# A spectral filter and two MLPs in one kernel: the filter's units regrouped, most of the last transform moved into its loop, weight preparation re-timed

## The chip, the core and the metric

The kernel runs on one core of a Trainium2 chip. The core has a matrix engine (PE, TensorE), three elementwise engines (DVE or VectorE, ACT or ScalarE, POOL or GpSimd) and a queue engine (SP, SyncE) that here issues every DMA. Each engine works through its own list of instructions in order and waits where an operand is not there yet. The metric is the device time of one execution in microseconds (us); the profile's span runs from its first to its last instruction.

## What is computed

```
X = rfft(x, axis=1);  Y = X * (filt_r + 1j*filt_i);  y = irfft(Y, n=3008)   # x: 2 x 3008 x 256
h = y.reshape(6016, 256) @ moe_w_in;  g = maximum(0.01*h, h);  z = g @ moe_w_out   # 256 -> 2048 -> 256
h = z @ moe2_w_in;  r = maximum(h, 0);  out = (r*r) @ moe2_w_out                   # 256 -> 2048 -> 256
```

All of it is float32. The weights arrive as 64-bit words.

## The kernel before, in words

**Filter.** The 3008-point transform is done as 47 x 64 by matrix products. The data go in 32 *units*, each 16 channels of one of the two batches. The loop over s (lines 680 to 723) is a software pipeline, one unit per step: `load_x` (DMA), `stage_a` (PE product `pa`), `stage_r` (DVE transpose `bin`), `stage_b` (PE product `px`), `stage_s` (ACT copies `xc`, DVE multiplies by `fr`), `stage_2` (POOL multiplies by `fi`), `stage_y` (for units in `SWAP` the two products are added, on DVE for those in `SWAP_V`, else on POOL), `stage_i` (PE product `zps`, two of them for units that are not in `SWAP`), `stage_t` (DVE transpose into `zin`). The sign of `fi` is applied in place, by `sign_f` on DVE or POOL, or by `sign_k` on ACT. `units` (line 529) alternates the batches, so each `fr` tile serves two neighbouring units.

**Last transform.** It has 32 *items* (h, j): half h of the channels and 376 tokens j. `stage_o` does four PE products `pi`, `stage_w` copies the result to the first tokens' tile `x0` or to `xo`, from where SP writes it to the DRAM tensor `xt`. An item can run when all units of its half and batch are in `zin`. Before, the 16 items of the first half run in the loop from step 19 on and in its drain, the other 16 in `fill()` (lines 743 to 756) after the loop's buffers are given back.

**MLPs.** A *macro* is a pair of token blocks (512 or 480 tokens each), a *panel* 256 of the 2048 hidden units; one *step* is one panel of one macro. There are 96 steps, 48 in each layer. `up(i, part)` does the seven block products of a step in three passes each (21 PE instructions `ph`), `down` 24 more (`py`). Of a step's results DVE forms `v`, `u` and three `h` in a fixed order, ACT applies the activation twice (`g` and the rounded `gp`), POOL forms the rest `gp` as a difference. PE's list runs one step ahead with `up`: the product into a `ph` bank that `u` or `v` reads is waited for.

**Side work.** Two tick clocks set where other work stands in the engines' lists: `begin(clock, steps, table, start)` gives each named operation a due tick, `tick` records what is due. The loop ticks "F" four times a step; `up` ticks "M" (and F) eight times a step, so a step of the MLP is `TM = 8` ticks. On them lie: `narrow_w`, which turns a panel's 64-bit words into float32 (ten DVE operations, lines 213 to 228, with `add`, `sums` and the split into high and low halves on POOL, DVE and ACT), for panels 0 to 3 of layer one at `STARTS` (clock F), panels 4 to 7 at `STARTS_1`, and the eight panels of layer two from `STARTS_2` on, one every 32 ticks (clock M; these go to DRAM, and `split_w` reads them back in layer two, late by `LATE`); and `macro_steps`, which prepares the operands of the next macro: `load`, the differences `sum0` to `sum3` (POOL, line 333), the halves `hi_` (ACT) and `lo_` (line 344; five on DVE, two on POOL), from 24 ticks before the macro's first step to 2 behind it. The macros of layer one begin at ticks 32, 128, 192, 256 and 320 (a first macro is split in two visits, the second of which reloads its operands).

```
for d in [d for d in due[c] if d[0] <= clock[c]]:
    due[c].remove(d)
    d[1]()
```

Of the kernel before, what the change touches and what calls it, by code (L numbers as in the profile page):

```python
# [9 lines left out]
F32 = mybir.dt.float32  # L10
# [10 lines left out]
NB = 2  # L21
# [18 lines left out]
WARM = 12  # L40


SWAP = (3, 7, 9, 11, 12, 15, 16, 17, 18, 19, 20, 21, 22, 23, 24, 25, 26, 27, 28, 29, 30, 31)
SWAP_V = (3, 16, 17, 18, 20, 21, 25, 26, 27, 29, 30)


FI = ((2, 4, 2), (4, 8, 2), (8, 16, 7))
SGN = (1, 2)
SIGN = ((4, 8, 4, 4), (8, 16, 9, 3))

H0 = 3
DRAIN = (2, 2, 2, 2)
FILLS = 13
OUT_V = (0, 1, 2, 3, 4, 5, 6, 7, 9, 15)

FIN = (0, 0)

TM = 8
STARTS = (-10, 34, 72, 112)
STARTS_1 = (0, 16, 32, 56)
STARTS_2 = 80


HALF = 4
# [13 lines left out]
    low1=17, load1=17, add1=18, out_o=19, out_i=26,  # L82
)

LATE = 20
SPLIT_W = dict(load=16, hi_i=18, hi_o=19, lo_i=20, lo_o=23)
FIRST = dict(
    hi_t1=-13, hi_b11=-13, lo_t1=-13, lo_b11=-13, sum1=-12, hi_b21=-12, lo_b21=-11, hi_t2=-11, lo_t2=-10, sum2=-9,
    sum3=-8, hi_t3=-8, lo_t3=-7, hi_t4=-7, lo_t4=-6, hi_b22=-6, lo_b22=-5,
)  # L90
MACRO = dict(
    load=-24, sum0=-16, sum1=-15, sum2=-12, hi_b11=-11, sum3=-9, hi_b21=-8, hi_t2=-8, lo_b11=-8, lo_t2=-8,
# [9 lines left out]
    N2=(),  # L102
    S=("lo_o",),
    M=("lo_b11", "lo_b21", "lo_t2", "lo_t3", "lo_t4"),
    M0=("lo_t2", "sum1", "sum2", "sum3", "lo_t4"),
)


# [43 lines left out]
def fft_filter_then_two_mlps(  # L152
# [343 lines left out]
    with ExitStack() as fctx:  # L496
# [5 lines left out]
        ps_z = actx.enter_context(tc.tile_pool(name="ps_z", bufs=1, space=PS))  # L502
        ps_x = actx.enter_context(tc.tile_pool(name="ps_x", bufs=2, space=PS))
        ps_a = actx.enter_context(tc.tile_pool(name="ps_a", bufs=3, space=PS))
        xin_p = actx.enter_context(tc.tile_pool(name="xin", bufs=4, side="right"))
        f_p = actx.enter_context(tc.tile_pool(name="flt", bufs=4, side="right"))
        s_p = actx.enter_context(tc.tile_pool(name="fs", bufs=3, side="right"))

# [17 lines left out]
        for _ in range(WARM):  # L526
            nc.tensor.matmul(warm_ps, warm[:, :P], warm, start=True, stop=True)

        units = [(b, q) for q in range(NU) for b in range(NB)]
        fr_sb = {}  # L530
        z10 = [z1_p.tile([P, P * NJ], F32, tag="z10", name="fi0")]
        fi_sb = [
# [10 lines left out]
            xin[s] = t  # L543

        def load_fr(q):
            fr_sb[q] = f_p.tile([P, UC, NK], F32, tag="fr", name="fr")
            nc.sync.dma_start(fr_sb[q], fr[:, q * UC : (q + 1) * UC, :])

        def load_fi(q0, q1):
# [81 lines left out]
                )  # L631
            pis[h, j] = pi

        def stage_w(h, j, eng):
# [6 lines left out]
            if h == 0:  # L641
# [27 lines left out]
        nc.sync.dma_start(cs, c_cs)
        load_w(0, 0, 1)  # L670
        load_x(3)
        load_fr(1)
        load_fi(1, 2)
        load_x(4)
        nc.sync.dma_start(dd, c_dd)
        n = len(units)
        h0 = w0 = 0
        for k, t in enumerate(STARTS):
            begin("F", narrow_w(0, k, f"F{k}"), NARROW_F, t)
        for s in range(n + 4):  # L680
# [12 lines left out]
            tick("F")
# [29 lines left out]
            tick("F")
        while w0 < NO:
            if h0 < NO:
                stage_o(0, h0, ps_a, "pa")
# [14 lines left out]
        h1 = iter(range(NO))  # L741

        def fill():
            j = next(h1)
            stage_o(1, j, ps_y, f"py{j % 4}")
            stage_w(1, j, nc.vector if j in OUT_V else nc.scalar)
# [102 lines left out]
```

## Time and profile before

| | |
|---|---|
| time, median of 3 runs | 1163.13 us (1162.51 to 1165.67) |
| the profiled execution: its time / its span | 1165.77 us / 1163.1 us |
| PE busy | 1117.3 us, 96% of the span |
| PE weight load, DVE, ACT, POOL busy | 883.9, 652.8, 649.8, 765.6 us |
| mean granted TensorE clock | 0.993 of full speed |
| DMA | 80.12 MB in all, mean 69 GB/s |

A busy share is a mean over stages with different limits. The filter and its last transform take the first 131 us, the two MLPs the rest. A row of the timeline gives the start, the time and the instruction, merged with its like (x6: six of them), and in brackets how long the engine had been idle and what ended that.

### The profile page before, as it was taken

To read this page: it belongs to the slowest core of one execution; us is meant where nothing else is said; L and a number is where in the kernel's file an instruction comes from. 1 tells how busy PE (TensorE), PEld (TensorE's weight loads), DVE (VectorE), ACT (ScalarE), POOL (GpSimd) and SP (SyncE) were. 2 spreads that over 40 slices of the span, in tenths; PEclk is the share of its full clock that TensorE was granted. 3 is DMA by queue.
4 is the path that set the end of the run, shared out by engine and by line. 5 is a ranking of instruction groups with operands and counts; after the bars stand their busy time and mean duration, and the time that the engine had idled before them with its cause. 6 is when DMAs were issued, how large, how long until landed. Compare 5 with 4: busy or idle time off the path is not lost.

```text
span 1163.1 us, 14072 instructions
## 1 busy us (share of the span) xinstructions
PE 1117.3 (96%) x4800; PEld 883.9 (76%) x4800; DVE 652.8 (56%) x870; ACT 649.8 (56%) x1209; POOL 765.6 (66%) x616
## 2 busy tenths in 40 slices
PE   7899978999899899899899999999999999999998
PEld 3466866888688688678688788788888788788887
DVE  6899788565854854855744643533534434435432
ACT  3855456554554554555555765655656555656554
POOL 3785598777757857756767876745647547557544
PEclk9999999999999999999999999999999999999999
DMA  7653712116022022023032030010100200200100
GB/s 229 189 158 117 265 54 78 55 56 239 20 82 95 23 84 86 19 80 96 1 111 87 28 106 38 31 40 1 63 11 1 71 1 1 71 1 1 37 1 34
DMA packets 35238, 80.12 MB, mean 69 GB/s; under 512 B 4544, under 2 KB 14880, under 8 KB 35040
## 3 DMA queue, kind: packets, MB, share of 16 engines
q1 hardware_dynamic: 35168, 79.25, 20.6%
q8 instruction: 37, 0.61, 0.2%
q14 instruction: 33, 0.27, 0.1%
HBM read 51.31 MB, written 27.92 MB: 68 GB/s over the span
## 4 chain that ended last, share of the span: by engine, by line
PE 76%; DVE 10%; ACT 4%; issue 4%; POOL 3%; DMA 2%; SPq 0%; DVEq 0%; POOLq 0%; ACTq 0%
PE py L463 38%; PE ph L368 34%; DVE xop L344 3%; PE pi L629 1%; POOL gp L391 1%; ACT g L381 1%; PE pa L571 1%; PE px L583 1%; DMA xin<-in_x 1%; ACT xop L338 1%; DVE u L402 1%; DVE wm L213 1%; DVE wi L222 1%; PE zps L613 1%; ACT gp L382 1%
## 5 line engine op out<-in xcount | busy, mean ns | idle before, releaser
L391 POOL TENSOR_TENSOR gp<-g,gp 128x512 fp32r<-128x512 f32 (+1 forms) x384 | 502.6, 1318 | 340.0 <-ACT gp L382 102.4
L463 PE MATMUL py<-gp,wao 128*128 128x512 f32 (+1 forms) x1152 | 287.8, 391 | 0.3 <-POOL gp L391 0.3
L463 PE MATMUL py<-gp,wbo 128*128 128x512 f32 (+1 forms) x1152 | 288.0, 392 | 0.0
L368 PE MATMUL ph<-xop,wai 128*128 128x512 f32 (+1 forms) x1008 | 259.2, 394 | 20.5 <-DVE v L402 11.6
L368 PE MATMUL ph<-xop,wbi 128*128 128x512 f32 (+1 forms) x1008 | 254.9, 391 | 8.7 <-DVE u L402 8.7
L463 PEld LDWEIGHTS py<-gp,wbo 128*128 128x128 f32 x1152 | 217.2, 189 | 48.1 <-POOL gp L391 0.2
L463 PEld LDWEIGHTS py<-gp,wao 128*128 128x128 f32 x1152 | 216.5, 188 | 48.5 <-POOL gp L391 0.7
L368 PEld LDWEIGHTS ph<-xop,wai 128*128 128x128 f32 x1008 | 187.7, 188 | 69.3 <-DVE v L402 14.1
L368 PEld LDWEIGHTS ph<-xop,wbi 128*128 128x128 f32 x1008 | 187.5, 187 | 53.4 <-DVE u L402 10.4
L381 ACT ACTIVATE g<-h 128x512 f32<-128x512 f32 (+1 forms) x144 | 88.9, 617 | 133.5 <-DVE h L402 128.9
L402 DVE TENSOR_TENSOR u<-ph,p 128x512 f32<-128x512 f32 (+1 forms) x96 | 65.0, 677 | 156.4 <-PE ph L368 156.4
L402 DVE TENSOR_TENSOR v<-ph,p 128x512 f32<-128x512 f32 (+1 forms) x96 | 65.0, 677 | 136.8 <-PE ph L368 64.7
L389 ACT ACTIVATE g<-h 128x512 f32<-128x512 f32 (+1 forms) x144 | 89.0, 618 | 85.6 <-DVE h L398 84.1
L387 ACT ACTIVATE r<-ph 128x512 f32<-128x512 f32 (+1 forms) x48 | 28.2, 587 | 106.5 <-PE ph L368 106.5
L390 ACT ACTIVATE gp<-h 128x512 fp32r<-128x512 f32 (+1 forms) x144 | 87.4, 607 | 0.0
L382 ACT ACTIVATE gp<-h 128x512 fp32r<-128x512 f32 (+1 forms) x144 | 87.3, 607 | 0.0
L381 ACT ACTIVATE g<-ph 128x512 f32<-128x512 f32 (+1 forms) x48 | 28.2, 587 | 97.9 <-PE ph L368 97.9
L398 DVE CUSTOM_DVE_ANT_0 h<-ph,p 128x512 f32<-128x512 f32 (+1 forms) x48 | 32.6, 680 | 86.8 <-PE ph L368 86.8
L402 DVE TENSOR_TENSOR h<-ph,p 128x512 f32<-128x512 f32 (+1 forms) x48 | 32.7, 680 | 73.7 <-PE ph L368 73.7
L421 ACT ACTIVATE p<-ph 128x512 f32<-128x512 f32 (+1 forms) x96 | 54.7, 570 | 1.5 <-PE ph L368 1.5
L601 POOL TENSOR_TENSOR t<-xc,fi 128x384 f32<-128x384 f32 x32 | 35.8, 1121 | 21.1 <-ACT xc L591 16.5
L344 DVE TENSOR_TENSOR xop<-x,xop 128x512 fp32r<-128x512 f32 (+1 forms) x33 | 41.0, 1243 | 10.4 <-ACT xop L338 10.4
(200 smaller groups left out, 1146.3 us busy)
## 6 DMA issues: line engine op xcount, KB each, us to landing
wraw<-in_w SPq DMA_DIRECT2D x32, 512.0 KB
xin<-in_x SPq DMA_DIRECT2D x32, 160.0 KB
xt<-xo SPq DMA_DIRECT2D x26, 188.0 KB
yt<-o SPq DMA_DIRECT2D x16, 256.0 KB
x<-yt SPq DMA_DIRECT2D x4, 1024.0 KB
out<-o SPq DMA_DIRECT2D x16, 256.0 KB
w<-wi SPq DMA_DIRECT2D x8, 448.0 KB
wi<-w SPq DMA_DIRECT2D x8, 448.0 KB
```

The source lines that it names most:

```text
L344: eng.tensor_tensor(t[:, 1, :n], x_f32[v][name], t[:, 0, :n].bitcast(F32), ALU.subtract)
L368: nc.tensor.matmul(ph[:, :n], w[:, i, k], x[:, j, :n], start=(first and a == 0), stop=(a == 2), skip_group_check=True)
L381: nc.scalar.activation(g[:, :n], h[:, :n], AF.Prelu, alpha=0.01)
L382: nc.scalar.activation(t[:, 0, :n], h[:, :n], AF.Prelu, alpha=0.01)
L389: nc.scalar.activation(g[:, :n], h[:, :n], AF.Square)
L390: nc.scalar.activation(t[:, 0, :n], h[:, :n], AF.Square)
L391: nc.gpsimd.tensor_tensor(t[:, 1, :n], g[:, :n], t[:, 0, :n].bitcast(F32), ALU.subtract)
L398: nc.vector._custom_dve(dve_ops.TENSOR_ADD_SAT, out=t[:, :n], in0=ph[:, :n], in1=s[:, :n], s0=F32_MAX, s1=0.0)
L402: nc.vector.tensor_tensor(t[:, :n], ph[:, :n], s[:, :n], ALU.add)
L421: nc.scalar.activation(p1[:, :n], ph[0][:, :n], AF.Copy)
L463: nc.tensor.matmul(acc[c, t][:, :n], w[:, j, 2 * f + c], g[:, k, :n], start=(p == p0 and f == t and a == 0), stop=(p == p1 - 1 and f != t ...
L601: nc.gpsimd.tensor_tensor(t2, xc, fi_of(units[s][1], units[s][1] + 1), ALU.mult)
```

## The change

Units are ordered by four groups of eight: half h, then batch b, then the eight units q of that half (`GU = 8`). So the first group's items can run from step 11 on, and 24 of the 32 items lie in the loop, one a step; `FILLS = 8` remain behind it. Each `fr` tile is now needed by units eight steps apart (nine buffers instead of four) and `fr` and `fi` of the first eight units are loaded one unit at a time. The first weight panel is no longer loaded ahead of everything, and `STARTS` is 20 ticks later for panel 0. Three of the first macro's differences move into the loop on DVE. In the MLPs `STARTS_1`, `STARTS_2` and `LATE` are new numbers. The count of PE instructions stays the same.

```
-SWAP_V = (3, 16, 17, 18, 20, 21, 25, 26, 27, 29, 30)
+SWAP = (9, 10, 11) + tuple(range(13, 32))
+SWAP_V = (10, 15, 18, 21, 24, 27, 30)
-FI = ((2, 4, 2), (4, 8, 2), (8, 16, 7))
-SGN = (1, 2)
-SIGN = ((4, 8, 4, 4), (8, 16, 9, 3))
+FI = ((8, 12, 5), (12, 16, 6))
+SIGN_K = 8
+SGN = (1, 3, 5, 7)
+SIGN = ((8, 16, 9, 3),)
+GU = 8
-DRAIN = (2, 2, 2, 2)
-FILLS = 13
-OUT_V = (0, 1, 2, 3, 4, 5, 6, 7, 9, 15)
+FILLS = 8
+OUT_V = (8, 10, 11, 13, 15)
-STARTS = (-10, 34, 72, 112)
-STARTS_1 = (0, 16, 32, 56)
-STARTS_2 = 80
+STARTS = (10, 42, 75, 108)
+STARTS_1 = (0, 32, 48, 64)
+STARTS_2 = 96
-LATE = 20
+LATE = (12, 12, 12, 20, 20, 20, 20, 20)
...
-    M0=("lo_t2", "sum1", "sum2", "sum3", "lo_t4"),
+    M0=("lo_t2", "lo_t4"),
...
-        units = [(b, q) for q in range(NU) for b in range(NB)]
+        units = [(b, q) for h in range(2) for b in range(NB) for q in range(h * GU, (h + 1) * GU)]
...
-        load_w(0, 0, 0)
         load_x(0)
+        nc.sync.dma_start(cb, c_cb)
         load_x(1)
...
+            if s < n - 3 and units[s + 3][0] == 0:
+                q = units[s + 3][1]
+                load_fr(q)
+                if q < SIGN_K:
+                    load_fi(q, q + 1)
+            if s in (1, 3):
+                load_w(0, 0, s // 2)
...
-            if s > n // 2 + H0 and w0 < h0:
-                stage_w(0, w0, nc.scalar)
+            if w0 < h0:
+                stage_w(*items[w0], nc.scalar)
                 w0 += 1
                 if w0 == 5:
                     sum_macro(FIRST_V, 0, nc.gpsimd)
+                if w0 - NO in (4, 5, 6):
+                    sum_macro(FIRST_V, w0 - NO - 3, nc.vector)
...
-            if s >= n // 2 + H0:
-                for k in range(1 if s < n else DRAIN[s - n]):
-                    if h0 < NO:
-                        stage_o(0, h0, ps_a, "pa")
-                        h0 += 1
+            if s >= GU + H0 and h0 < len(items) - FILLS:
+                stage_o(*items[h0], ps_a, "pa")
                 h0 += 1
...
-            begin("M", split_w(1, p, "S", {}), SPLIT_W, ((NM - 1) * NP + p) * TM + (LATE if p >= NWA - 1 else 0))
+            begin("M", split_w(1, p, "S", {}), SPLIT_W, ((NM - 1) * NP + p) * TM + LATE[p])
```

The lines of the changed kernel are one off (L402 is L403 there). Three places in the engines' lists follow.

**PE, from the last steps of the loop to the first products `ph` of the MLP.** `pi` are the items, four products each. Before:

```order
L571 MATMUL pa<-xin,ra 128x512
L583 MATMUL px<-bin,cb 128x384
L613 MATMUL zps_122<-t_968,ci 128x16x24
L629 MATMUL pi<-dd,zin_119 128x128 x4
L583 MATMUL px<-bin,cb 128x384
L613 MATMUL zps_123<-t_997,ci 128x16x24
L629 MATMUL pi<-dd,zin_119 128x128 x8
L613 MATMUL zps_121<-t_1024,ci 128x16x24
L629 MATMUL pi<-dd,zin_119 128x128 x4
L613 MATMUL zps_122<-t_1048,ci 128x16x24
L629 MATMUL pi<-dd,zin_679 128x128 x32
L629 MATMUL pi<-dd,zin_120 128x128 x32
```

and now:

```order
L572 MATMUL pa<-xin,ra 128x512
L584 MATMUL px<-bin,cb 128x384
L614 MATMUL zps_122<-t_1019,ci 128x16x24
L630 MATMUL pi<-dd,zin_732 128x128 x4
L584 MATMUL px<-bin,cb 128x384
L614 MATMUL zps_123<-t_1046,ci 128x16x24
L630 MATMUL pi<-dd,zin_732 128x128 x4
L614 MATMUL zps_121<-t_1075,ci 128x16x24
L630 MATMUL pi<-dd,zin_732 128x128 x4
L614 MATMUL zps_122<-t_1100,ci 128x16x24
L630 MATMUL pi<-dd,zin_732 128x128 x4
L630 MATMUL pi<-dd,zin_120 128x128 x32
```

Of the 64 products of 16 items behind the last `zps`, 32 are left (and 4 just ahead of them); the others stand in the loop's steps.

**DVE, in step 3, ahead of the macro that begins at tick 32,** from `v` to `u` of one step. `xop` are the low halves of the next macro's operands; `wb`, `wi` and `wm` belong to panel 5 of layer one. Before:

```order
L402 TENSOR_TENSOR v<-ph,p_1576 128x512
L344 TENSOR_TENSOR xop<-x,xop 128x512
L344 TENSOR_TENSOR xop<-xs,xop 128x512
L217 SCALAR_TENSOR_TENSOR wb__1561<-wraw_1405,wb__1561 128x512
L222 TENSOR_SCALAR wi_1596<-wb__1561 128x512
L344 TENSOR_TENSOR xop<-x,xop 128x512
L228 SCALAR_TENSOR_TENSOR wm<-wraw_1405,wi_1596 128x512
L402 TENSOR_TENSOR u<-ph,p_1576 128x512
```

and now:

```order
L403 TENSOR_TENSOR v<-ph,p_1556 128x512
L345 TENSOR_TENSOR xop<-x,xop 128x512
L345 TENSOR_TENSOR xop<-xs,xop 128x512
L345 TENSOR_TENSOR xop<-x,xop 128x512
L403 TENSOR_TENSOR u<-ph,p_1556 128x512
```

The three operations on panel 5 have left this gap. At the macros that begin at ticks 128, 192, 256 and 320 the same happens with the panels of layer two: before, `L344`, `L344`, `L222`, `L344`, `L228` stood between `v` and `u`, now only the three `L345`.

**POOL, ahead of the macro that begins at tick 128.** `xs` and `x` (480 wide) are the macro's differences, `wi` and `wo` the layer-two panel's sums. Before:

```order
L391 TENSOR_TENSOR gp<-g,gp 128x512 x7
L333 TENSOR_TENSOR xs<-x 128x480
L333 TENSOR_TENSOR xs<-x,xs 128x480
L391 TENSOR_TENSOR gp<-g,gp 128x512 x2
L333 TENSOR_TENSOR x<-x 128x480
L391 TENSOR_TENSOR gp<-g,gp 128x512 x2
L333 TENSOR_TENSOR xs<-x,xs 128x480
L344 TENSOR_TENSOR xop<-xs,xop 128x480
```

and now:

```order
L334 TENSOR_TENSOR xs<-x 128x480
L242 TENSOR_TENSOR wi_2536<-wi_2536 128x128
L243 TENSOR_TENSOR wi_2536<-wi_2536 128x128
L244 TENSOR_TENSOR wi_2536<-wi_2536 128x128
L245 TENSOR_TENSOR wi_2536<-wi_2536 128x128
L334 TENSOR_TENSOR xs<-x,xs 128x480
L392 TENSOR_TENSOR gp<-g,gp 128x512
L237 TENSOR_TENSOR wo_2645<-wb__2609,wm 128x512
L392 TENSOR_TENSOR gp<-g,gp 128x512
L334 TENSOR_TENSOR x<-x 128x480
L392 TENSOR_TENSOR gp<-g,gp 128x512 x2
L334 TENSOR_TENSOR xs<-x,xs 128x480
```

A panel's five POOL operations of line 237 and lines 242 to 245 now stand among the macro's differences.

## Rows read from the trace of the kernel before

**Rows 1.** Page, part 1: busy time, share, instructions.

```profile
PE 1117.3 (96%) x4800; PEld 883.9 (76%) x4800; DVE 652.8 (56%) x870; ACT 649.8 (56%) x1209; POOL 765.6 (66%) x616
```

**Rows 2.** Timeline of PE, 110 to 200 us.

```profile
114.33 16.84 PE L629 MATMUL pi<-dd,zin 128*128 128x128 f32 x128 [1.48 <-DVE zin L622]
130.93 3.74 PE L368 MATMUL ph<-xop,wai 128*128 128x512 f32 x15
...
163.94 2.96 PE L463 MATMUL py<-gp,wao 128*128 128x512 f32 x12
172.57 2.92 PE L368 MATMUL ph<-xop,wai 128*128 128x512 f32 x6 [5.66 <-DVE u L402]
...
185.20 2.97 PE L463 MATMUL py<-gp,wao 128*128 128x512 f32 x12
...
196.41 2.96 PE L463 MATMUL py<-gp,wao 128*128 128x512 f32 x12
```

**Rows 3.** Timeline of DVE, 155 to 196 us.

```profile
162.23 0.69 DVE L402 TENSOR_TENSOR v<-ph,p 128x512 f32<-128x512 f32 x1 [1.42 <-ACT p L421]
...
163.70 1.77 DVE L344 TENSOR_TENSOR xop<-xs,xop 128x512 fp32r<-128x512 f32 x1
...
171.84 0.68 DVE L402 TENSOR_TENSOR u<-ph,p 128x512 f32<-128x512 f32 x1
```

**Rows 4.** What PE waited for, 200 to 600 us: total, times, longest.

```profile
PE ph L368 <- DVE v L402: 8.8, 4, 2.3
PE ph L368 <- DVE u L402: 8.7, 4, 2.4
```

**Rows 5.** Timeline of PE at the macro of tick 128, 285 to 322 us.

```profile
290.93 2.96 PE L463 MATMUL py<-gp,wbo 128*128 128x512 f32 x12
...
301.44 2.97 PE L463 MATMUL py<-gp,wbo 128*128 128x512 f32 x12
...
316.66 4.42 PE L463 MATMUL py<-gp,wbo 128*128 128x512 f32 x12
```

**Rows 6.** Timeline of DVE at the same place.

```profile
299.86 0.68 DVE L402 TENSOR_TENSOR v<-ph,p 128x512 f32<-128x512 f32 x1
...
303.06 1.52 DVE L222 TENSOR_SCALAR wi<-wb__2736 128x512 int32<-128x512 int32 x1
...
305.68 0.68 DVE L402 TENSOR_TENSOR u<-ph,p 128x512 f32<-128x512 f32 x1
```

**Rows 7.** Timeline of PE at a change of macro in layer two, 741 to 762 us.

```profile
745.79 2.96 PE L463 MATMUL py<-gp,wbo 128*128 128x512 f32 x12
...
756.79 2.96 PE L463 MATMUL py<-gp,wao 128*128 128x512 f32 x12
```

**Rows 8.** Timeline of PE in the filter, 0 to 112 us.

```profile
6.63 3.75 PE L571 MATMUL pa<-xin,ra 94*128 94x512 f32 x4 [2.51 <-DMA xin<-in_x]
...
39.82 1.02 PE L571 MATMUL pa<-xin,ra 94*128 94x512 f32 x2
...
67.58 1.02 PE L571 MATMUL pa<-xin,ra 94*128 94x512 f32 x2
...
102.68 1.02 PE L571 MATMUL pa<-xin,ra 94*128 94x512 f32 x2
```

**Rows 9.** Windows: busy us of each engine (instructions), clock, DMA share, GB/s.

```profile
0.00:30.00 30.00, 23.43 (x57) 11.86 (x58) 19.93 (x34) 10.35 (x23) 12.54 (x16) 1.00 0.80 233
30.00:40.00 10.00, 9.36 (x28) 4.90 (x27) 6.59 (x11) 8.52 (x23) 8.34 (x9) 1.00 0.94 290
```

**Rows 10.** Windows, the same columns: eleven steps of the loop, each with an item.

```profile
67.60:102.70 35.10, 34.63 (x157) 22.53 (x156) 33.77 (x55) 19.05 (x38) 25.53 (x25) 1.00 0.45 142
```

**Rows 11.** Timeline of DVE in the filter: one operation at two places.

```profile
45.28 0.64 DVE L217 SCALAR_TENSOR_TENSOR wb__444<-wraw,wb__444 128x512 int32<-128x512 int32 x1
...
80.91 1.75 DVE L217 SCALAR_TENSOR_TENSOR wb__773<-wraw,wb__773 128x512 int32<-128x512 int32 x1
```

**Rows 12.** Timeline of POOL, 78 to 84 us.

```profile
80.53 1.58 POOL L333 TENSOR_TENSOR xs<-x 128x512 f32<-128x512 f32 x1
```

More of the change, by code (lines that the diff above doesn't have):

```diff
@@ L40 @@
 WARM = 12
-SWAP = (3, 7, 9, 11, 12, 15, 16, 17, 18, 19, 20, 21, 22, 23, 24, 25, 26, 27, 28, 29, 30, 31)
-SWAP_V = (3, 16, 17, 18, 20, 21, 25, 26, 27, 29, 30)
-FI = ((2, 4, 2), (4, 8, 2), (8, 16, 7))
-SGN = (1, 2)
-SIGN = ((4, 8, 4, 4), (8, 16, 9, 3))
+SWAP = (9, 10, 11) + tuple(range(13, 32))
[5 more added lines that the diff above has]
+GU = 8
 H0 = 3
-DRAIN = (2, 2, 2, 2)
-FILLS = 13
-OUT_V = (0, 1, 2, 3, 4, 5, 6, 7, 9, 15)
+FILLS = 8
+OUT_V = (8, 10, 11, 13, 15)
 FIN = (0, 0)
 TM = 8
-STARTS = (-10, 34, 72, 112)
-STARTS_1 = (0, 16, 32, 56)
-STARTS_2 = 80
+STARTS = (10, 42, 75, 108)
+STARTS_1 = (0, 32, 48, 64)
+STARTS_2 = 96
 HALF = 4
@@ L83 @@
 )
-LATE = 20
+LATE = (12, 12, 12, 20, 20, 20, 20, 20)
 SPLIT_W = dict(load=16, hi_i=18, hi_o=19, lo_i=20, lo_o=23)
 FIRST = dict(
-    hi_t1=-13, hi_b11=-13, lo_t1=-13, lo_b11=-13, sum1=-12, hi_b21=-12, lo_b21=-11, hi_t2=-11, lo_t2=-10, sum2=-9,
-    sum3=-8, hi_t3=-8, lo_t3=-7, hi_t4=-7, lo_t4=-6, hi_b22=-6, lo_b22=-5,
+    hi_b11=-8, hi_t2=-8, lo_b11=-8, lo_t2=-7, hi_t1=-7, lo_t1=-6, hi_b21=-5, lo_b21=-4, hi_t3=-4, lo_t3=-3, hi_t4=-2,
+    lo_t4=-1, hi_b22=-1, lo_b22=0,
 )
@@ L504, in fft_filter_then_two_mlps @@
         ps_a = actx.enter_context(tc.tile_pool(name="ps_a", bufs=3, space=PS))
-        xin_p = actx.enter_context(tc.tile_pool(name="xin", bufs=4, side="right"))
+        xin_p = actx.enter_context(tc.tile_pool(name="xin", bufs=5, side="right"))
         f_p = actx.enter_context(tc.tile_pool(name="flt", bufs=4, side="right"))
@@ L545, in load_fr @@
         def load_fr(q):
-            fr_sb[q] = f_p.tile([P, UC, NK], F32, tag="fr", name="fr")
+            fr_sb[q] = f_p.tile([P, UC, NK], F32, tag="fr", name="fr", bufs=GU + 1)
             nc.sync.dma_start(fr_sb[q], fr[:, q * UC : (q + 1) * UC, :])
@@ L632, in stage_o, with stage_w @@
             pis[h, j] = pi
-        def stage_w(h, j, eng):
+        def stage_w(h, j, eng, pi_in_loop=True):
             pi = pis.pop((h, j))[:, :, : 2 * N1]
@@ L640, in stage_w @@
                 return
-            if h == 0:
+            if pi_in_loop:
                 o = xw_p.tile([P, TO], F32, tag="xo", name="xo")
@@ L659, in fft_filter_then_two_mlps @@
         x0 = load_macro(FIRST_V, load=False).rearrange("p k t n -> p k (t n)")
-        load_w(0, 0, 0)
         load_x(0)
+        nc.sync.dma_start(cb, c_cb)
         load_x(1)
-        nc.sync.dma_start(cb, c_cb)
-        nc.sync.dma_start(sg, c_sg)
         load_fr(0)
         load_fi(0, 1)
+        nc.sync.dma_start(sg, c_sg)
         load_x(2)
@@ L669, in fft_filter_then_two_mlps @@
         nc.sync.dma_start(cs, c_cs)
-        load_w(0, 0, 1)
-        load_x(3)
         load_fr(1)
         load_fi(1, 2)
-        load_x(4)
+        load_x(3)
+        load_fr(2)
+        load_fi(2, 3)
         nc.sync.dma_start(dd, c_dd)
         n = len(units)
+        items = [(h, j) for h in range(2) for j in range(NO)]
         h0 = w0 = 0
@@ L680, in fft_filter_then_two_mlps @@
         for s in range(n + 4):
-            if 2 <= s < n - 3:
+            if 1 <= s < n - 3:
                 load_x(s + 3)
+            if s < n - 3 and units[s + 3][0] == 0:
[5 more added lines that the diff above has]
+                load_w(0, 0, s // 2)
             if s < n:
@@ L707, in fft_filter_then_two_mlps @@
                 stage_i(s - 3)
-            if s % 2 == 0 and s // 2 + 2 < NU:
-                load_fr(s // 2 + 2)
             for i, (a, b, t) in enumerate(FI):
@@ L712, in fft_filter_then_two_mlps @@
                     load_fi(a, b)
-            if s % 2 == 0 and s // 2 < FI[1][0]:
-                sign_f(s // 2)
+            if 1 <= s <= SIGN_K:
+                sign_f(s - 1)
             for q0, q1, t, c in SIGN:
@@ L717, in fft_filter_then_two_mlps @@
                     sign_k(q0, q1, k)
-            if s >= n // 2 + H0:
-                for k in range(1 if s < n else DRAIN[s - n]):
-                    if h0 < NO:
-                        stage_o(0, h0, ps_a, "pa")
-                        h0 += 1
[L723 to L726, printed above, removed]
+            if s >= GU + H0 and h0 < len(items) - FILLS:
+                stage_o(*items[h0], ps_a, "pa")
                 h0 += 1
-            stage_w(0, w0, nc.scalar)
-            put()
-            w0 += 1
             tick("F")
@@ L740, in fft_filter_then_two_mlps, with fill @@
         ps_y = ctx.enter_context(tc.tile_pool(name="ps_y", bufs=1, space=PS, reuse_waits="tile"))
[L741 to L746, printed above, removed]
+        def fill(h, j):
+            stage_o(h, j, ps_y, f"py{j % 4}")
+            stage_w(h, j, nc.vector if j in OUT_V else nc.scalar, False)
             put()
             tick("F")
-        for _ in range(NO - FILLS):
-            fill()
         clock["M"] = -FILLS
@@ L754, in fft_filter_then_two_mlps @@
         begin("M", {name: lambda name=name: save_op(FIRST_V, name) for name in ORDER}, SAVE, 0)
-        for _ in range(FILLS):
-            fill()
+        for h, j in items[h0:]:
+            fill(h, j)
             tick("M")
```

## The prediction

> **What bounds the kernel now.** I read the page's busy shares first: PE is busy 96% of the span [rows 1], so only what keeps PE from its products can be won, and the question is where PE stands still. The timeline of PE shows two parts. The first `ph` of the MLPs begins at 130.93 us [rows 2]; until then PE serves the filter. From there to the end at 1163.1 us PE has a fixed list: the block of twelve `py` comes once a step, and in a quiet stretch two of them are 10.51 us apart (290.93 and 301.44) [rows 5]. So a lost microsecond shows as a longer distance between two such blocks, and the reader can find every loss of the MLPs that way. Three kinds stand out. Step 3: from 163.94 to 185.20, 21.26 us, and 11.21 us to the next at 196.41 [rows 2]. The change of macro at tick 128: from 301.44 to 316.66, 15.22 us [rows 5]. And the waits of PE from 200 to 600 us: four times for `v` and four times for `u`, 17.5 us together [rows 4], that is one pair at each of the four macros of layer one that begin at ticks 128 to 320. In layer two, where the same operands are prepared but no panel is narrowed, a change of macro costs 11.00 us instead of 10.50 (745.79 to 756.79) [rows 7].
>
> What PE waits for there is DVE's list. At the change of macro DVE ends `v` at 300.54 and reaches `u` at 305.68, with three halves `xop` and two narrowing operations between them [rows 6]. In step 3 it is 162.92 to 171.84, with three halves and three narrowing operations [rows 3], and PE's wait of 5.66 us ends with that `u` [rows 2]. It is a matter of order: the narrowing of the panels that start at tick 16 and at ticks 112, 176, 240 and 304 falls on the ticks of a macro's halves.
>
> **The change, part by part.**
>
> *Layer two's panels 16 ticks later (`STARTS_2`).* A panel's DVE work lies 7 to 17 ticks behind its start, every 32 ticks; a macro's DVE halves lie from 8 ticks before its first step to its first tick. With starts at 96, 128 and so on, the panels work at ticks 103 to 113, 135 to 145, ..., and the halves at 120 to 128, 184 to 192, ...: no panel meets one. The order of DVE agrees, only the three halves stay between `v` and `u`. Today's loss is 15.22 less 10.51, 4.7 us, at each of four places, 18.8 us; the waits alone say 17.5, so the rest of a longer step is mostly these waits. What remains is bounded by the 0.5 us of layer two below and by all 4.7 above, if POOL takes DVE's place (rival 2). I take 0.7, near the lower row, since the list is then that of layer two but for POOL's panel work: **16.0 us gained** (0 to 16.8).
>
> *Layer one's panels 5 to 7 later (`STARTS_1`).* Step 3 and the next cost 10.75 and 0.7 us over 10.5, together 11.45. Behind `v` (end 162.92) three halves remain; at the dearest price of one there, 1.77 us [rows 3], they end at 168.2, and `u` begins 3.6 us earlier than today. That alone would cut the wait of 5.66 to 2.0; the narrowing operations of the next gap go too. So the gain is between 3.6 and 11.45. POOL is as full there as before, so I do not take the upper end: **9.0 us**.
>
> *`LATE`.* The first three panels of layer two are read back 12 ticks later, still a whole step or more ahead of their use at tick 384. Nothing waits for them; zero, unless ACT's and POOL's work for panel 2 meets that macro's differences, which I hold under 1 us by the 0.5 of rows 7.
>
> *Weights not first in the queue.* PE's first `pa` waits 2.51 us for `xin` behind the 512 KB of `wraw` [rows 8]. With `xin` ahead the wait is between 0 and 2.51; I take 2.0 us gained at the start.
>
> *The units in groups.* The twelfth unit's `pa` (step 11) is at 39.82 today [rows 8]. In the new order the data ahead of it in SP's queue are 12 `xin` of 192 KB, 8 `fr` and 8 `fi` of 197 KB, the other 8 units' `fi` (1.57 MB), 1.05 MB of weights and 0.33 MB of constants: 8.4 MB. The queue moved 233 GB/s over the first 30 us, 7.0 MB, and 290 GB/s after that [rows 9], so 8.4 MB are there at 34.8 us. I put step 11 at 36.5 (31 if the queue runs at 290 from 2 us on; 42 if data and a halved clock cost more than today).
>
> *The items in the loop.* They are no new work, only moved: a step with an item takes 3.19 us today (67.58 to 102.68, eleven steps) [rows 8], of which PE is busy 34.63 of 35.10 us and DVE 33.77 [rows 10]. From step 11 to the last `pa` (step 31) are 20 steps, 63.8 us: 100.3. From the last `pa` to the run of items behind the loop is 11.65 us today (102.68 to 114.33), the last units' way through ACT, POOL and DVE transposes; I leave it. Then 8 items at 16.60 us for 16 (114.33 to 130.93) [rows 2]: 8.3 us. Sum 120.25; two units that are not in `SWAP` now fall into steps with items, so I take 121. The operands of the first macro need five POOL halves there; the eight items cover them, as sixteen did, and without that cover the first `ph` would wait up to five times about 1.3 us less those 8.3, so nothing. **9.9 us gained** (130.93 less 121; 1 to 15).
>
> *Moved for nothing:* signs of `fi` from ACT to DVE and POOL (four short operations), three differences of the first macro, on DVE as before, from behind the loop into its steps 30 to 33: they lie beside PE while DVE's list keeps below a step's 3.19 us. DVE has 1.33 us left in eleven steps [rows 10], so this cover is thin; that is rival 1.
>
> **Sum.** 16.0 + 9.0 + 9.9 = 34.9 us: a span of 1128.2, an execution of 1130.9 against the profiled one's 1165.77. The median of the runs is 1163.13, 2.6 below the profiled execution, so the forecast for the median is **1128 us**.
>
> **Rivals.**
>
> 1. *The filter gains nothing.* DVE, not PE, sets the loop. For it: 33.77 of 35.10 us busy [rows 10], and the same narrowing work stays in the loop. Against it: today's loop already runs so with an item a step, and the items are ACT's and PE's work. If step 11 comes at 39.8 and each step costs 0.3 more, the first `ph` begins near 130: 16.0 + 9.0 + 1 = 26, 1137 us.
>
> 2. *POOL takes DVE's place.* The panel's POOL work now stands among the macro's differences (the order shows it), and a late difference holds up ACT's and DVE's halves. A DVE operation of line 217 took 0.64 us with POOL idle and 1.75 us from 80.91, while POOL worked from 80.53 to 82.11 [rows 11, 12]: the two slow each other. The three halves would again take over 5 us, and behind late differences keep 3.5 of the 4.7 us each: 4.8 gained instead of 16.0; step 3 keeps all but 3.6. 9.9 + 4.8 + 3.6 = 18.3, 1145 us. Against it: layer two has the same halves and differences and loses 0.5 [rows 7]. The Trainium skill, SBUF — State Buffer, section "Who interferes with whom", says that a DVE operation with two SBUF inputs and a GpSimd operation that reads SBUF exclude each other for a whole instruction. By that rule this change moves a collision rather than removing it, and the time would be this rival's; rows 11 and 12 agree that the second comer waits.
>
> 3. *Slower.* The same blocking inside the loop. A panel has ten narrowing operations in some 8.25 steps; if each rose from 0.64 to 1.75 us, a step would cost 1.35 us more on DVE, 3.07 + 1.35 = 4.4 us, and 20 such steps 24 us: the first `ph` at 145, 14 us later than today. If the macros gain nothing either, 1177 us. It decides from 3.19 + 9.9/20 = 3.7 us a step on: from there the front part loses. Against it: today's eleven steps carry a whole panel and a part of the next at 3.07.
>
> 4. *No change.* The panels could still fall on the halves; the order of DVE says no.
>
> **Chances.** Forecast 0.65, rival 1 0.16, rival 2 0.12, rival 3 0.04, rival 4 0.03. The forecast's own bounds (front part 1 to 15, the four macros 14 to 16.8, step 3 from 3.6 to 11.45) give 1120 to 1144; rivals 1 and 2 lie at 1137 and 1145. Range **1115 to 1145**. Faster by over 0.3% (3.5 us, about what a measurement of this kernel can tell from no change): 0.93; within: 0.03; slower: 0.04.
>
> **What would show it.** In the profile after: first `pa` near 4.6 us; first `ph` at 121 (rival 1: 130); blocks of twelve `py` at most 11.3 us apart at the four changes of macro, and no wait for `u` or `v` over 1 us there (rival 2: waits for `u`, with POOL busy without a gap); one step near 13 us instead of 21.26 at step 3. Wrong is the reasoning if the total comes right while the macros' steps stay at 15 us.

## The result, and the profile after

| | before | after |
|---|---|---|
| median of the runs | 1163.14 us (1162.51 to 1165.67) | 1138.05 us (1137.12 to 1139.09) |
| the profiled execution: its time / its span | 1165.77 / 1163.1 us | 1139.09 / 1137.0 us |
| first `ph` of the MLPs | 130.93 us | 131.97 us |
| from there to the end | 1032.2 us | 1005.0 us |

The ratio is 0.9781, interval 0.9763 to 0.9798: 25.1 us faster, where the forecast's sum had 34.9. The time lies within the range. The last two lines of the table divide the span: the MLPs gained 27.1 us (25.0 forecast), and the filter, forecast to gain 9.9 us, lost 1.0. The 27.1 us are far above the scatter; the 1.0 us is not, since another execution of the changed filter has its first `ph` at 129.61 us (`front_only`, below).

Part 1 of the page of the changed kernel answers to [rows 1]:

```profile
PE 1112.3 (98%) x4800; PEld 881.0 (77%) x4800; DVE 647.1 (57%) x863; ACT 642.8 (57%) x1190; POOL 767.8 (68%) x622
```

The counts of the engines have hardly moved: the same work in a span that is 26.1 us shorter.

**The MLPs.** What PE waited for between 200 and 600 us in the changed kernel (total, times, longest) answers to [rows 4]:

```profile
PE ph L369 <- DVE v L403: 1.3, 5, 0.4
PE ph L369 <- DVE u L403: 0.3, 1, 0.3
```

Of 17.5 us of waits 1.6 are left. Step 3, from the timeline of PE of the changed kernel, answers to [rows 2] (a bracket gives how long PE had stood idle, and for what):

```profile
131.97 3.75 PE L369 MATMUL ph<-xop,wai 128*128 128x512 f32 x15
...
164.82 2.96 PE L464 MATMUL py<-gp,wao 128*128 128x512 f32 x12
168.51 1.70 PE L369 MATMUL ph<-xop,wai 128*128 128x512 f32 x6 [0.72 <-DVE u L403]
...
176.34 2.96 PE L464 MATMUL py<-gp,wao 128*128 128x512 f32 x12
```

The blocks of twelve `py` are 11.52 us apart where they were 21.26, and PE's wait for `u` has shrunk from 5.66 to 0.72 us. The long wait had a second price that the forecast did not name. In the kernel before, behind it, the window (start:end, length, busy us of PE, PEld, DVE, ACT and POOL, granted clock, DMA share, GB/s) is

```profile
170.00:176.00 6.00, 3.43 (x8) 2.76 (x9) 4.31 (x6) 2.67 (x5) 5.72 (x5) 0.50 0.26 87
```

At a granted clock of 0.50 the first six `ph` took 2.92 us [rows 2], now 1.70; in the changed kernel the clock is 1.00 there. The timeline of DVE of the changed kernel at the same place answers to [rows 3]:

```profile
163.10 0.69 DVE L403 TENSOR_TENSOR v<-ph,p 128x512 f32<-128x512 f32 x1 [3.96 <-ACT p L422]
163.71 0.74 DVE L345 TENSOR_TENSOR xop<-x,xop 128x512 fp32r<-128x512 f32 x1
164.37 1.78 DVE L345 TENSOR_TENSOR xop<-xs,xop 128x512 fp32r<-128x512 f32 x1
166.07 1.77 DVE L345 TENSOR_TENSOR xop<-x,xop 128x512 fp32r<-128x512 f32 x1
167.77 0.68 DVE L403 TENSOR_TENSOR u<-ph,p 128x512 f32<-128x512 f32 x1
```

From the end of `v` to the start of `u` DVE needs 3.98 us (163.79 to 167.77) where it needed 8.92: only the three halves are left in the gap. At the macro that begins at tick 128 the timeline of PE of the changed kernel answers to [rows 5]:

```profile
292.42 2.96 PE L464 MATMUL py<-gp,wbo 128*128 128x512 f32 x12
...
302.71 2.97 PE L464 MATMUL py<-gp,wbo 128*128 128x512 f32 x12
...
312.60 0.92 PE L369 MATMUL ph<-xop,wai 128*128 128x480 f32 x3 [0.26 <-DVE v L403]
313.36 2.79 PE L464 MATMUL py<-gp,wao 128*128 128x480 f32 x12
...
324.43 2.80 PE L464 MATMUL py<-gp,wao 128*128 128x480 f32 x12
...
334.33 2.80 PE L464 MATMUL py<-gp,wao 128*128 128x480 f32 x12
```

The step of the change takes 10.29 us instead of 15.22. A panel still costs something where it lies now, in the steps behind the change of macro: the longest distance there is 11.07 us (313.36 to 324.43), where the next step, as wide (480 tokens) and quiet, takes 9.90.

**The filter.** The timeline of PE of the changed kernel answers to [rows 8]; the last lines answer to the first of [rows 2]:

```profile
4.03 3.13 PE L572 MATMUL pa<-xin,ra 94*128 94x512 f32 x4
...
12.00 1.10 PE L572 MATMUL pa<-xin,ra 94*128 94x512 f32 x2 [2.22 <-DMA xin<-in_x]
...
21.78 1.10 PE L572 MATMUL pa<-xin,ra 94*128 94x512 f32 x2 [2.26 <-DMA xin<-in_x]
...
41.88 1.02 PE L572 MATMUL pa<-xin,ra 94*128 94x512 f32 x2
...
110.34 1.02 PE L572 MATMUL pa<-xin,ra 94*128 94x512 f32 x2
...
118.98 1.63 PE L614 MATMUL zps<-t,ci 128*128 128x384 f32 x2 [2.55 <-DVE t L609]
...
124.44 7.78 PE L630 MATMUL pi<-dd,zin 128*128 128x128 f32 x64 [0.41 <-DVE zin L623]
```

The wait of 2.51 us ahead of the first `pa` is gone, but two waits for `xin` of 2.2 and 2.3 us come behind it. Step 11 is at 41.88 us, 2 us later than before, and step 31 at 110.34: a step with an item takes 3.42 us on average (68.46 over 20). The average hides two kinds of step: twelve of the twenty take 3.08 to 3.12 us, and four take 4.94, 4.03, 4.41 and 4.19. In those four PE waits for transposes of DVE; between 41.88 and 110.34 us the waits of PE (total, times, longest) are

```profile
PE px L584 <- DVE bin L579: 2.7, 3, 1.1
PE pi L630 <- DVE zin L623: 0.8, 1, 0.8
```

Later in the front PE waits 2.55 us for DVE's sum `t`.

The windows show what DVE was doing. The columns are the stretch, its length, the busy us (instructions) of PE, PEld, DVE, ACT and POOL, the granted clock, the DMA share and GB/s. Before:

```profile
0.00:22.00 22.00, 16.99 (x40) 8.85 (x40) 14.65 (x25) 4.93 (x8) 9.27 (x14) 1.00 0.79 227
22.00:42.00 20.00, 17.80 (x49) 8.90 (x50) 12.29 (x22) 15.88 (x39) 11.92 (x12) 1.00 0.84 254
42.00:102.00 60.00, 56.93 (x214) 33.61 (x213) 56.74 (x94) 38.44 (x77) 45.67 (x43) 0.97 0.46 143
...
sum 132.00, PE 119.24 PEld 75.94 DVE 109.42 ACT 72.73 POOL 82.58; mean PE 29.81 PEld 18.98 DVE 27.36 ACT 18.18 POOL 20.64
```

and after:

```profile
0.00:22.00 22.00, 16.10 (x39) 8.78 (x40) 8.21 (x15) 3.79 (x6) 5.18 (x9) 0.92 0.70 216
22.00:42.00 20.00, 17.82 (x49) 8.77 (x49) 19.51 (x32) 6.48 (x13) 13.91 (x14) 1.00 0.91 266
42.00:102.00 60.00, 56.39 (x246) 35.69 (x245) 55.58 (x81) 39.78 (x80) 48.52 (x47) 1.00 0.52 159
...
sum 132.00, PE 116.97 PEld 74.41 DVE 109.69 ACT 65.31 POOL 86.83; mean PE 29.24 PEld 18.60 DVE 27.42 ACT 16.33 POOL 21.71
```

DVE works 109.4 us of the first 132 in the one and 109.7 in the other. (PE's own sums are larger, 119.2 and 117.0 us: it is not the sum that makes DVE the one to look at, but the waits above.) Before, 14.65 us of it lay in the first 22, while data arrived: the narrowing of panel 0, whose weights led the queue. The change has put those weights behind the units' data, so DVE has 8.21 us there, is full in the next 20 us (19.51), and keeps 55.58 of 60 in the loop. PE does 32 instructions more from 42 to 102 us than before (246 and 214), which is what the new order does give it, but the first `ph` does not come earlier by the 8.3 us of items that no longer stand at the end.

### The profile page after: what moved, and what is told of

It reads as the page before. It is cut to its first block, busy times and chain, and to the rows that moved or that the text cites. A ratio compares the mean times of both kernels' runs of the same rounds, so it can differ in the third digit from the quotient of the medians.

```text
span 1137.0 us, 14038 instructions
## 1 busy us (share of the span) xinstructions
PE 1112.3 (98%) x4800; PEld 881.0 (77%) x4800; DVE 647.1 (57%) x863; ACT 642.8 (57%) x1190; POOL 767.8 (68%) x622
## 4 chain that ended last, share of the span: by engine, by line
PE 81%; DVE 8%; DMA 3%; issue 3%; POOL 3%; ACT 2%; SPq 1%; POOLq 0%; DVEq 0%; ACTq 0%
PE py L464 41%; PE ph L369 36%; DMA xin<-in_x 2%; PE pi L630 1%; DVE xop L345 1%; DVE wm L214 1%; POOL xop L345 1%; DVE h L403 1%; PE pa L572 1%; POOL gp L392 1%; PE px L584 1%; DMA x<-xt 1%; PE zps L614 1%; DVE zin L623 1%; DVE u L403 1%
## 5 line engine op out<-in xcount | busy, mean ns | idle before, releaser
L403 DVE TENSOR_TENSOR v<-ph,p 128x512 f32<-128x512 f32 (+1 forms) x96 | 65.0, 677 | 138.2 <-PE ph L369 67.5
L403 DVE TENSOR_TENSOR u<-ph,p 128x512 f32<-128x512 f32 (+1 forms) x96 | 64.9, 676 | 130.5 <-PE ph L369 130.5
L403 DVE TENSOR_TENSOR h<-ph,p 128x512 f32<-128x512 f32 (+1 forms) x48 | 32.7, 680 | 72.9 <-PE ph L369 72.9
L345 DVE TENSOR_TENSOR xop<-x,xop 128x512 fp32r<-128x512 f32 (+1 forms) x33 | 47.0, 1425 | 10.4 <-ACT xop L339 6.8
L602 POOL TENSOR_TENSOR t<-xc,fi 128x384 f32<-128x384 f32 x32 | 34.9, 1095 | 15.2 <-DVE fi L564 10.9
```

The source lines that it names most:

```text
L345: eng.tensor_tensor(t[:, 1, :n], x_f32[v][name], t[:, 0, :n].bitcast(F32), ALU.subtract)
L403: nc.vector.tensor_tensor(t[:, :n], ph[:, :n], s[:, :n], ALU.add)
L602: nc.gpsimd.tensor_tensor(t2, xc, fi_of(units[s][1], units[s][1] + 1), ALU.mult)
```

## The experiments

Two questions: do the MLP terms alone make the gain, and what holds the filter at 130 us? Each ratio stands against executions of the kernel before that were taken with the variant; their median lay between 1161.4 and 1163.1 us, so two times out of different experiments can differ by 1 to 2 us for that alone.

**The MLP tables alone** (`mlp_only`): the kernel before with `STARTS_1`, `STARTS_2` and `LATE` of the change.

```
-STARTS_1 = (0, 16, 32, 56)
-STARTS_2 = 80
+STARTS_1 = (0, 32, 48, 64)
+STARTS_2 = 96
-LATE = 20
+LATE = (12, 12, 12, 20, 20, 20, 20, 20)
```

> The kernel before with the new STARTS_1, STARTS_2 and LATE alone; the filter, its loop and the last transform as before. Theory A (the gain is the panels' DVE work leaving the gaps of the macros' halves): the first ph stays at 131 us, the MLPs give back the 27 us that they gave in the change, 1136 us. Theory B (the MLPs gained because the front part hands over with DVE and POOL free, and with three differences done earlier): under 10 us gained, 1153 us or more.

Measured: 1136.33 us, ratio 0.9778 (0.976 to 0.9796). Three tables of numbers make the whole gain; the first `ph` is at 129.79 us, and from there the MLPs take 1005.2 us of the span, as in the changed kernel.

**Each table by itself.** `starts1_only` has the first line of that diff alone, `starts2_only` the other two.

> The kernel before with the new STARTS_1 alone. Theory A: only the step from 163.94 to 185.20 us shrinks, to about 12 us, 9 to 11 us gained, 1153 us; the four later changes of macro stay at about 15 us. Theory B: nothing, 1163 us.

> The kernel before with the new STARTS_2, and LATE, which keeps the last panel's buffers apart from the read-back. Theory A: the four changes of macro at ticks 128 to 320 fall from about 15 to about 10.9 us, 16 to 19 us gained, 1146 us; step 3 stays at 21 us. Theory B: nothing, 1163 us. If POOL takes DVE's place there, under 6 us gained.

Measured: 1150.41 us, 0.9905 (0.9872 to 0.9938), and 1146.95 us, 0.9868 (0.9846 to 0.9891), against 1161.72. The gains, 11.3 and 14.8 us, add up to 26.1 where both together gave 25.4: two separate losses (the first gain is known to about 4 us only, by its interval). With `STARTS_1` alone the blocks of step 3 are 11.29 us apart and the four later changes of macro stay at 15.1 to 15.5; PE's waits from 200 to 600 us there still hold

```profile
PE ph L368 <- DVE u L402: 8.7, 4, 2.4
```

which is the line of [rows 4] unchanged. With `STARTS_2` alone step 3 stays at 21.8 us and the four changes take 10.3 to 10.7.

**The new filter alone** (`front_only`): the changed kernel with the old tables in the MLPs.

```
-STARTS_1 = (0, 32, 48, 64)
-STARTS_2 = 96
+STARTS_1 = (0, 16, 32, 56)
+STARTS_2 = 80
-LATE = (12, 12, 12, 20, 20, 20, 20, 20)
+LATE = (0, 0, 0, 20, 20, 20, 20, 20)
```

> The changed kernel with STARTS_1, STARTS_2 and LATE set back: the new front part alone. Theory A: the first ph stays at 132 us, and the MLPs lose their 27 us again, 1165 us, no better than the kernel before. Theory B: the MLPs keep most of their gain, 1138 to 1145 us.

Measured: 1164.63 us, 1.0022 (1.0012 to 1.0032). By itself the regrouped filter gains nothing; it is 0.1 to 0.3% slower. Step 3 is back at 21.26 us and the four changes at 15.1 to 15.5. This execution has the same filter as the changed kernel, and its timeline of PE has

```profile
39.53 1.02 PE L572 MATMUL pa<-xin,ra 94*128 94x512 f32 x2
...
129.61 3.74 PE L369 MATMUL ph<-xop,wai 128*128 128x512 f32 x15
```

where the changed kernel has 41.88 and 131.97. Step 6 is at 22.51 us here and at 24.65 there; from step 6 to the first `ph` the two agree within 0.3 us (107.10 and 107.32).

**DVE without the narrowing** (`no_narrow`): the changed kernel, in which panels 0 to 3 leave out eight of their ten narrowing operations on DVE and the two additions behind them (eight for the four panels, four of them on POOL), so that their weights are not the reference's. PE's list is untouched.

```
+        bare = kind in ("F0", "F1", "F2", "F3")
...
+            if bare:
+                return
```

> The changed kernel, but panels 0 to 3 leave out eight of the ten DVE narrowing operations and the add (their weights are not the reference's); loads, ACT and the split stay. About 29 us of DVE work leave the loop. Theory C (DVE sets the filter's loop, PE and the queue do not): the first ph comes at 117 to 120 us instead of 132, about 1125 us. Theory D (the data of the first eight units and PE's own work set it): step 11 stays near 42 us and the first ph at 128 us or later, 1135 us or more.

Measured: 1126.73 us, 0.9691 (0.9675 to 0.9708), some 11 us under the changed kernel. The windows of this kernel, same columns as above, and the first `ph` of its PE timeline:

```profile
42.00:102.00 60.00, 60.00 (x270) 39.85 (x269) 44.75 (x70) 41.08 (x83) 42.32 (x45) 1.00 0.50 151
...
sum 132.00, PE 123.57 PEld 82.05 DVE 92.57 ACT 73.25 POOL 84.75; mean PE 30.89 PEld 20.51 DVE 23.14 ACT 18.31 POOL 21.19
```

```profile
119.55 3.75 PE L381 MATMUL ph<-xop,wai 128*128 128x512 f32 x15
```

Up to the first `ph` DVE has worked 82.8 us, where it was 109.7 in the changed kernel, and PE is busy 60.00 of 60 us in the loop. Step 11 is at 37.60 and step 31 at 101.04: 3.17 us a step, where the forecast had said 36.5 and 3.19, and the first `ph` is 1.5 us off its 121. The forecast described a loop that PE sets. In the changed kernel the narrowing makes the loop longer than that. It is DVE's work for the most part; the omission takes POOL from 48.52 to 42.32 us in the same 60 as well, so that DVE by itself is not separated from POOL here.

**The same omission in the old filter** (`old_front_no_narrow`): `mlp_only`, with the same operations of panels 0 to 3 left out.

> The kernel with the old front part and the new starts, and the same eight narrowing operations and the add left out of panels 0 to 3 (their weights are not the reference's). If the new order of units and items is worth something once DVE has room, the first ph comes later here than the 119.6 us of the new front part without them, at 122 us or more, 1129 us. If PE's work is simply the same in both orders and DVE hid nothing but itself, it comes at 117 to 121 us, 1125 to 1127 us.

Measured: 1127.5 us, 0.9699 (0.9683 to 0.9715).

```profile
122.19 3.75 PE L380 MATMUL ph<-xop,wai 128*128 128x512 f32 x15
```

The old order gains some 9 us from it too (1136.33 to 1127.50). This lies between the two outcomes that were named. Free of DVE's load, the new order's first `ph` is 2.6 us ahead of the old one's, but the medians are 0.8 us apart and the intervals overlap. So even with DVE out of the way the regrouping saves little; that the items simply cost PE the same in the loop and behind it is likely, but these runs do not separate it from the rest.

**Less or later work for DVE in the loop.** Five more variants of the changed kernel.

`fills16` has 16 items in the loop and 16 behind it, with the three differences behind it as well:

```
-FILLS = 8
+FILLS = 16
...
```

> The changed kernel with 16 instead of 24 items in the loop and 16 behind it (the three differences move behind the loop with them). Theory C: the items in the loop stand in DVE's shadow, so eight more behind it cost PE's full 8 x 0.97 us, less the 2.9 us of differences that leave DVE's chain: 5 to 8 us slower, 1143 to 1146 us. Theory D (PE sets the loop): the same work either way, 1138 us.

Measured: 1141.48 us, 0.9818 (0.9803 to 0.9832), first `ph` 134.38. It is 3.4 us slower than the changed kernel, 4.3 by the ratios, between the two theories. The traces say why. From step 11 to step 26 both have an item a step, and both take 51.9 us. From step 26 to step 31, without items here, it is 12.60 us against 16.54 with them: the five items cost 0.8 us a step there, most of what PE needs for one. Behind the last `pa` it is 29.94 us against 21.63. So about half of the eight items' time is paid in the loop; what is saved comes from the last steps, in which PE waits anyway without them (up to 2.2 us for `t` here, and the granted clock is 0.50 from 114 to 120 us). The items do not simply lie in DVE's shadow, and PE does not simply set the loop.

`sums_late` leaves the 24 items where they are and moves only the three differences of the first macro (1.49, 0.69 and 0.67 us on DVE, at 111.12, 115.37 and 119.92 in the changed kernel) behind the loop, on DVE still, where they lay before the change:

```
+    sum1=-8, sum2=-8, sum3=-7,
...
-                if w0 - NO in (4, 5, 6):
-                    sum_macro(FIRST_V, w0 - NO - 3, nc.vector)
```

> The changed kernel with the three differences of the first macro done on DVE in the first two of the eight items behind the loop instead of in steps 30 to 33. Theory C: DVE's chain to the last unit's transpose is 2.9 us shorter, the first ph at about 129 us, 1135 us, unless the first macro's halves now come late. Theory D: 1138 us.

Measured: 1135.92 us, 0.977 (0.9755 to 0.9784), first `ph` 129.96. The median is 2.1 us lower than that of the changed kernel, 1.3 us by the ratios, and the intervals overlap. In the traces the way from the last `pa` to the first `ph` falls from 21.63 to 20.82 us: 0.8 us, of the 2.85 us of DVE's time that it takes out of the last steps; the granted clock, which falls there in the changed kernel, stays at 1.00. Behind the loop the three take 0.68, 0.69 and 0.69 us, under PE's items.

`panel0_early` loads panel 0 between the first units' data and narrows it while data arrive:

```
-STARTS = (10, 42, 75, 108)
+STARTS = (-2, 42, 75, 108)
...
+        load_w(0, 0, 0)
...
```

> The changed kernel with panel 0's words loaded between the first units' data and its narrowing 12 ticks earlier (the load of panel 1 stays where it was), so that its DVE work lies where DVE waits for data in the changed kernel, before 22 us. Theory C: 3 to 6 us of DVE work leave the loop, the first ph at 126 to 129 us, 1132 to 1135 us. Theory D: the units' data come later by the 1.05 MB, nothing or 2 us slower.

Measured: 1137.10 us, 0.9778 (0.9763 to 0.9792); first `ph` 128.91 in the profiled execution, 3.1 us earlier, but the medians differ by 1 us, and the ratios hardly at all. In the trace the way from step 6 to step 31 is 3.2 us shorter (82.50 against 85.69). Step 6, however, comes at 24.79 us, where the executions that load the data first (the changed kernel, `front_only`, `sums_late`, `fills16`) have it at 22.51 to 24.65: with the weights ahead in the queue a wait of PE for `xin` of 3.92 us stands at the start.

`combo` is the last two together, and `combo_pool` moves the four additions of panels 1 to 3 that DVE does to POOL on top of that.

> The changed kernel with panel 0's narrowing 12 ticks earlier and the three differences behind the loop, both at once. Theory C (DVE's list sets the front part): the two savings, 3 and 2 us, add up, the first ph at 127 us, 1133 to 1134 us, below the kernel that has the new starts alone (1136). If the two only trade places with other waits: 1136 us.

> As combo, and the four adds of panels 1 to 3 that DVE does (some 3.5 us) go to POOL. Theory C: another 1 to 3 us, 1131 to 1133 us. If POOL, some 80% busy in the loop, is by now as much of a bound as DVE: 1134 us or more.

Measured: 1136.31 us, 0.9781 (0.9765 to 0.9796), first `ph` 128.28; and 1134.73 us, 0.9768 (0.9752 to 0.9784), first `ph` 129.27. In `combo` the two savings add up in the trace, from step 6 on (103.18 us to the first `ph`, 4.1 less than in the changed kernel); in the median they do not, and its ratio is that of the change. `combo_pool` came out as had been expected for the case that POOL is by now as much of a bound as DVE: the 20 steps from step 11 on take 67.64 us, in `combo` 67.26. One step that took 4.19 us is at 3.26, but another has gone from 3.51 to 4.79, in which PE waits for POOL:

```profile
PE zps L615 <- POOL t L610: 1.4, 1, 1.4
```

`combo_pool` has the lowest median of the kernels that compute everything, but its interval overlaps with those of the change, of `mlp_only` and of `sums_late`. No version clearly beats the change.

## Why the prediction was right, and where it was wrong

**`STARTS_2`: 16.0 said, 14.8 measured alone** (0 to 16.8 given with the term; the range took 14 to 16.8). The mechanism is the one that was read: the panel's two operations stood between `v` and `u`, and the distance 15.22 became 10.29. That step costs nothing more, and the panels cost up to 1.2 us in the steps where they lie now (11.07 less the 9.90 of a quiet step of that width): of the 18.8 us some 4 remain, where 2.8 had been left.

**`STARTS_1`: 9.0 said, 11.3 measured alone,** at the upper end of 3.6 to 11.45. The step was expected near 13 us for the halves' dear price; it took 11.52. The halves were dear (1.78 and 1.77 us), but `v` to `u` in 3.98 us is early enough for PE, its second wait there (2.78 us for `v`) is gone, and so is the halved clock behind the first, for which the sum had no term.

**`LATE`: zero said.** It was not tried by itself; with `STARTS_2` the two give what `STARTS_2` was to give.

**The front part: 9.9 gained said, 1.0 lost.** Step 11 was put at 36.5 us and came at 41.88; 20 steps were put at 63.8 us and took 68.46; from the last `pa` to the run of items 11.65 us were left as they were, and it took 14.10. The eight items were put at 8.3 and took 7.53, because the 16.60 us of before held a stretch at half clock (0.50 from 116 to 118 us). Together 5.38 + 4.66 + 2.45 - 0.77 = 11.7 us, which is 131.97 less the 120.25 of the sum. The step that failed is the cover: "they lie beside PE while DVE's list keeps below a step's 3.19 us". The 1.33 us that DVE had left in eleven steps were read rightly as thin, and taken nevertheless, with the mean of eleven steps for all twenty. With the narrowing left out, the terms of the forecast came near what it had said (37.60, 3.17 us a step, 119.55).

Not all of the 5.38 us at step 11 is DVE's. By `front_only` (39.53) and `no_narrow` (37.60), 2.35 us of it differ between two executions of one and the same filter, 1.9 go with the narrowing, and 1.1 remain without it. The forecast counted what the loss of the weights' place at the head of the queue gives to PE (2.0 us, of which the later waits for `xin` took the most back), and not what it costs DVE: a whole panel's narrowing leaves a stretch in which DVE was waiting anyway and enters one in which it was full. `panel0_early` shows the size of that, 3.2 us in its trace.

That the front part gains nothing is **rival 1**, with 0.16: step 11 at 39.8 and 0.3 us more a step, first `ph` near 130, 1137 us. Measured: 41.88, 0.23 more a step, 131.97, 1138.05. The mechanism is in the main the rival's; that the totals are within 1.1 us is in part luck, since its MLP terms were 2 us low and its front part 2 us high. The forecast's range held because its lower bound for the front was a gain of 1 us. The steps of before would have pointed to the rival: the 3.19 us is a mean of eight steps of 3.08 or 3.09 us and three longer ones (3.72, 3.17 and 3.52), and in `old_front_no_narrow` those three take 3.08 or 3.09 as well. The cover had failed in places before the change.

**Rival 2** (POOL takes DVE's place) saw its signs and not its price. The timelines of DVE and of POOL in the changed kernel at the macro of tick 128:

```profile
289.17 0.69 DVE L403 TENSOR_TENSOR v<-ph,p 128x512 f32<-128x512 f32 x1 [2.11 <-PE ph L369]
289.78 0.84 DVE L345 TENSOR_TENSOR xop<-x,xop 128x480 fp32r<-128x480 f32 x1
290.54 1.74 DVE L345 TENSOR_TENSOR xop<-xs,xop 128x480 fp32r<-128x480 f32 x1
292.21 1.74 DVE L345 TENSOR_TENSOR xop<-x,xop 128x480 fp32r<-128x480 f32 x1
293.87 0.68 DVE L403 TENSOR_TENSOR u<-ph,p 128x512 f32<-128x512 f32 x1
```

```profile
290.04 3.39 POOL L392 TENSOR_TENSOR gp<-g,gp 128x512 fp32r<-128x512 f32 x2
293.40 1.64 POOL L334 TENSOR_TENSOR xs<-x,xs 128x480 f32<-128x480 f32 x1
```

Two of the three halves take 1.74 us, beside two `gp` of POOL, the first 0.84. The Trainium skill, SBUF — State Buffer, section "Who interferes with whom", says that two such operations exclude each other, and here the trace agrees that they slow each other. But `v` to `u` takes 4.01 us where 5.14 was too much, PE waits 0.4 us at most there, and DVE waits for no difference between 285 and 330 us. Of a collision that is moved, what counts is whether it is late for somebody.

**Rivals 3 and 4** fell: a step took 3.42 us, not the 4.4 of rival 3 nor its 3.7, and the macros gained what had been forecast; the panels have left the halves' ticks.

What stays open is why one and the same filter ends at different times; where it does so can be read. In four executions of the old front (before, `mlp_only`, `starts1_only`, `starts2_only`) the first `ph` was at 130.93, 129.79, 127.03 and 128.57 us. Step 20 comes at 65.2 to 68.0 us in them, the eleven steps behind it take 35.0 to 35.1 in all four, and the rest takes 28.3 where the granted clock falls in it (before, `starts2_only`) and 26.7 where it does not. So the scatter arises ahead of step 20, where PE waits 3.2 to 4.8 us for data and 1.9 to 5.2 us for DVE's `bin`, and from the clock. One profiled execution is therefore no measure of a front's gain of 2 us; the verdicts above rest on medians. That the three `LATE` values are needed to keep the read-back of panels 0 to 2 clear of the last panels of layer two was reasoned from the buffers and not tried.

## What to carry to other kernels

Look for repeated blocks in the timeline of the bounding engine and compare their distances; where periodic side work and periodic boundaries meet on an engine that works in order, shifting the phase of the one by a step or two can take the wait away, and is a change of a few numbers. Before work of the bounding engine is moved into a loop to fill its gaps, look at the loop step by step: which steps are longer than the engine's own work in them, and for which engine does it wait there? An average step hides them. Busy sums over the stage do not tell it (here PE's was larger than DVE's), and shares of a loop's best stretch are no cover for more of the same. Here, taking the work off the other engine ended the stage some 12 us earlier; moving it to another place or to a third engine changed the median by some 3 us at most.

## What was not expected of the hardware

PE's granted clock falls in the front, and not in every execution. In the changed kernel PE is busy 0.44 of the 2 us from 116 on, and then come (columns as above):

```profile
116.00:118.00 2.00, 0.44 (x4) 0.24 (x3) 1.97 (x5) 0.48 (x1) 1.92 (x4) 1.00 0.07 25
118.00:120.00 2.00, 1.01 (x2) 0.71 (x3) 2.00 (x4) 0.00 (x0) 0.51 (x1) 0.76 0.20 71
120.00:122.00 2.00, 2.00 (x9) 1.70 (x9) 1.97 (x4) 0.00 (x0) 1.31 (x1) 0.50 0.00 0
122.00:124.00 2.00, 2.00 (x12) 1.55 (x11) 2.00 (x4) 1.32 (x2) 0.19 (x1) 0.89 0.13 44
```

0.50 is the lower of its two levels, 1.2 GHz. The two products `zps` at 118.98 take 1.63 us, where a like pair takes 0.81 at 114.69. Another such fall comes from 12 to 18 us, behind 2 us in which PE stood still for `xin`. Up to the first `ph` the profiled executions of before (from 46 and from 114 us), `starts2_only`, `panel0_early` and `fills16` have two as well, `front_only`, `sums_late` and `combo` one, and `mlp_only`, `starts1_only`, `no_narrow`, `old_front_no_narrow` and `combo_pool` none. So a wait for DVE can cost PE something twice, in the filter as in step 3 of the MLPs, but it explains only a part of the differences between executions: `mlp_only` and `starts1_only` both had none, and their first `ph` are 2.8 us apart.
